# Sixteen copies of the conv's tap rows in DRAM, and half of a weight chunk copied from SBUF by SyncE

## The chip, the cores and the metric

The kernel runs on one core of a Trainium2 chip. The metric is the device time of one execution in microseconds. Several executions are taken and their median is told; one further execution is recorded by the hardware profiler, and every duration of a single instruction comes from that one.

## The reference

A light convolution is followed by a two-layer network with an ELU between its layers.

```python
# x: (8, 4096, 192), weight: (8, 7), w_in: (192, 2048), w_out: (2048, 192)
w = softmax(weight, axis=-1)                        # 8 heads, 7 taps
out[b, s, h, g] = sum_k w[h, k] * x_pad[b, s + k, h, g]   # causal, 24 channels per head
h = out.reshape(32768, 192) @ w_in
g = np.where(h > 0.0, h, np.exp(np.minimum(h, 0.0)) - 1.0)
return g @ w_out                                    # (32768, 192), float32
```

## The kernel before

The 32768 tokens are cut into 32 super-tiles of 1024 tokens (`s`), and each into two groups of 512. The hidden width of 2048 is cut into 16 blocks of 128 (`q`). A step `n = 16 s + q` makes, for both groups (`r` or `u` = 0, 1), the block `H` (three matmuls over 64 rows each, L748), its exponential (ACT, L542), a clamp (POOL, L470), and `gT = max(E - 1, H)` (DVE, L609). The products with `w_out` (L782) follow later in "rounds" that begin at step 12 and are spread among the `H` matmuls of later steps. The lists `ROUNDS`, `CONV_AT` and `EARLY_CONV` fix by hand where each piece stands, and `steps` is the order of all engines' work.

TensorE works on 64 rows at a time, in two row halves. So the weights `w_in` stand twice in SBUF: the rows 0 to 63 of the tile serve group 0, the rows 64 to 127, with the same content, serve group 1. The load runs in three chunks of columns, `WCOLS = ((0, 256), (256, 1024), (1024, 2048))`. Each chunk was loaded twice from DRAM, once for each half, with a cast from float32 to bf16. The chunk `k` counts on the semaphore `s_w[k]`, 16 for each load. `Q_PART` tells which chunk a block needs: the last one serves the blocks 8 to 15, so step 8 is the first to ask for it.

The conv of super-tile 0 is computed at the start from a separate load (`xf`, transposed by TensorE). From super-tile 1 on the conv is a matmul with a banded matrix `Tm` (L726): row `p` of `Tm` holds the taps of all heads, shifted by `p`. To build it, SyncE writes the tap rows into a DRAM tensor `conv_taps`, with zero rows around them (L799, L804), waits for both writes (`s_band`), and reads them back with a stride of -1 element per partition (L809). Before, `conv_taps` held two copies; the read took the partitions 0 to 63 from the one and 64 to 127 from the other:

```python
bass.AP(tensor=taps.tensor, offset=CW + TAP + KSIZE - 1,
        ap=[[(HEADS + 2) * CW - HP, 2], [-1, HP], [1, HEADS * CW]])
```

The conv of super-tile 1 is placed at steps 7 to 10, that of super-tile 2 at steps 13 and 14 (`EARLY_CONV`). Its first matmul waits for `s_band`, and for both halves of `xg`, the tokens of that super-tile. Its result goes through PSUM and ACT into `csb` (L520), and a transposing DMA on SyncE's queue turns it into `att`, the input of the `H` matmuls.

GpSimd's queue issues the casting loads at the start in this order: `w_in` chunk 0 twice, chunk 1 twice, chunk 2 twice, `xg` of super-tile 1 in two halves, `w_out`, `xg` of super-tile 2 in two halves. SyncE's queue issues the tap `weight`, one half of `xf`, the two writes of taps and the band's read; its next instruction is the transpose of super-tile 1. From super-tile 3 on the tokens come from a bf16 copy in DRAM (`x_cast`) that GpSimd's queue writes.

Of the kernel before, what the change touches and what calls it, by code (L numbers as in the profile page):

```python
# [8 lines left out]
BF16 = mybir.dt.bfloat16  # L9
# [3 lines left out]
P = 128  # L13
HP = 64
FC = 128
D = 192
HEADS = 8
KSIZE = 7
# [6 lines left out]
TAP = 6  # L25
# [16 lines left out]
CONV_AT = ((0, 1, 1, 0), (4, 1, 1, 1), (9, 2, 0, 0), (12, 2, 0, 1))  # L42
EARLY_CONV = ((7, 1, 0, 0), (8, 1, 0, 1), (9, 1, 1, 0), (10, 1, 1, 1), (13, 2, 0, 0), (14, 2, 0, 1))
OPS_CONV = 2
FIRST = {}
M_NS, R_NS, C_NS = 215.8, 82.5, 102.5
QUAD = 4
# [6 lines left out]
def bass_lightweight_conv__then__act_elu_kernel(  # L54
# [160 lines left out]
            t, half = divmod(n_half - 1, 2)  # L215
            previous[n_half // 2, n_half % 2, 0, g] = (t, half, 0, g)

    taps = nc.dram_tensor("conv_taps", (2 * (HEADS + 2) * CW,), BF16).ap()

    xb = nc.dram_tensor("x_cast", (NT, D), BF16).ap()  # L220

    with ExitStack() as stack:
# [6 lines left out]
        def sema(name):  # L229
            return stack.enter_context(nc.semaphore(name))  # L230
# [27 lines left out]
        ops = psum("ops", [P, 2, GS])  # L258

        s_w = [sema(f"s_w{i}") for i in range(4)]  # L260
        s_wd = sema("s_wd")
        s_xl = [sema(f"s_xl{i}") for i in range(2)]
        s_xh = sema("s_xh")
# [128 lines left out]
        @block.gpsimd  # L392
        def _gpsimd(g: bass.BassGpSimd):
            W = Waits(g)

            def load_x(s, part):
                g.dma_start(  # L397
                    xg[:, s % NXB, WPG * part : WPG * (part + 1), :],
                    bass.AP(
                        tensor=x_flat.tensor,  # L400
                        offset=(s * SUP + GS * part - PAD) * D,
                        ap=[[D, P], [TOK * D, WPG], [1, D]],
                    ),
                ).then_inc(s_x[s % NXB][part], 16)

            def pad_x(s):
                x_ready(W, s, 0)
                g.memset(xg[0:PAD, s % NXB, 0, :], 0.0).then_inc(s_z)

            def copy_x(s):  # L410
                W(s_cv, 4 * (s - NXB - 1) + 1)
                if s == NXB + 1:
                    g.dma_start(  # L413
                        xb[s * SUP - 8 : s * SUP, :], x_flat[s * SUP - 8 : s * SUP, :]
                    ).then_inc(s_xb[s % 2], 16)
                g.dma_start(  # L416
                    xb[s * SUP : (s + 1) * SUP, :].rearrange("(p t) d -> p (t d)", p=P),
                    x_flat[s * SUP : (s + 1) * SUP, :].rearrange("(p t) d -> p (t d)", p=P),
                ).then_inc(s_xb[s % 2], 16)

            def load_w_in(k, halves):
                c0, c1 = WCOLS[k]
                for r in halves:
                    g.dma_start(  # L424
                        w_in[HP * r : HP * (r + 1), :, c0:c1],
                        moe_w_in.rearrange("(p j) f -> p j f", j=3)[:, :, c0:c1],
                    ).then_inc(s_w[k], 16)

            W(s_one, 1)
            g.affine_select(  # L430
                out=ident[:],
                in_=ident[:],
                pattern=[[-1, P]],
                compare_op=ALU.is_equal,
                fill=0.0,
                base=0,
                channel_multiplier=1,
            ).then_inc(s_id)
            g.affine_select(  # L439
                out=sel[:].rearrange("p (r h c) -> p r h c", r=2, h=HEADS),  # L440
                in_=sel[:].rearrange("p (r h c) -> p r h c", r=2, h=HEADS),
                pattern=[[0, 2], [-1, HEADS], [0, 8]],
                compare_op=ALU.is_equal,
                fill=0.0,
                base=0,
                channel_multiplier=1,
            ).then_inc(s_id)
            W(s_wd, 16)
            load_w_in(0, (0, 1))
            load_w_in(1, (0, 1))  # L450
            load_w_in(2, (0, 1))
            load_x(1, 0)
            load_x(1, 1)
            g.dma_start(
                w_out.rearrange("p (q r) d -> p q (r d)", r=RUN),
                moe_w_out.rearrange("(q p r) d -> p q (r d)", p=FC, r=RUN),
            ).then_inc(s_w[3], 16)
            load_x(2, 0)
            load_x(2, 1)
            for n in range(NP):  # L460
                s, i = divmod(n, NQ)
                if i == X_PAD and s + 2 < NS and (s + 2) % SPB == 0:
                    pad_x(s + 2)
                if i == X_COPY and s and s + 3 < NS:
                    copy_x(s + 3)
                if n == X_LATE[0]:
                    copy_x(3)
                for u in range(2):
                    W(s_exp, 2 * n + u + 1)
                    g.tensor_scalar(  # L470
                        out=E[:, n % NE, u, :],
                        in0=E[:, n % NE, u, :],
                        scalar1=1.0,
                        scalar2=0.0,
                        op0=ALU.min,
                        op1=ALU.max,
                    ).then_inc(s_clp)
# [141 lines left out]
        def _tensor(pe):  # L619
# [75 lines left out]
            for x_, op in enumerate(steps):  # L695
# [42 lines left out]
                elif op[0] == "h":  # L738
                    _, n, r, j = op
                    s, q = divmod(n, NQ)  # L740
                    if n == 0:
                        W(s_ha, (1, 1, 2)[j])
                        W(s_hd, (0, 1, 2)[j])
                    if j == 0:
                        W(s_w[Q_PART[q]], 32)
                        W(s_att[s % 2], 16 * ((s + 1) // 2))
                        wait_bank()
                    ins = pe.matmul(  # L748
                        bank_of(op[:3]),
                        w_in[  # L750
                            HP * r : HP * (r + 1),
                            j,
                            RUN * FC * (q // RUN) + q % RUN : RUN * FC * (q // RUN + 1) : RUN,
                        ],
                        att[HP * r : HP * (r + 1), s % 2, j, 0:GS],
                        start=(j == 0),
                        stop=(j == 2),
                        tile_position=(HP * r, 0),
                    )
                    if j == 2:  # L760
                        ins.then_inc(s_h[r])
                else:
                    _, item, rt, g = op
                    t, half, q, kb, turned = item
                    acc = acc_of(op)
                    W(s_w[3], 16)
                    W(s_tt, 2 * (NQ * t + q) + g + 1)
                    at_end = acc[:2] == (last, 1)
                    if x_ in begins:
                        if at_end:  # L770
                            wait_bank()
                        elif acc in previous:
                            taken(W, previous[acc])
                        else:
                            W(s_ce, 2 * (OPS_CONV - 1) + g + 1)
                    elif steps[seen[acc]][2] != rt:
                        W(s_swap[1 - rt], ends_run[seen[acc]])
                    seen[acc] = x_
                    to = bank_of(("l",) + acc) if at_end else ops[:, g, :]
                    d0 = 0 if at_end else D * kb  # L780
                    t0 = 2 * P * half + P * kb
                    ins = pe.matmul(  # L782
                        to[:, d0 : d0 + D],
                        gT[HP * rt : HP * (rt + 1), t % NG3, q, g, t0 : t0 + P],
                        w_out[HP * rt : HP * (rt + 1), q, :],
                        start=(x_ in begins),
                        stop=(x_ in stops),
                        tile_position=(HP * rt, 0),
                    )
                    if x_ in ends_run:  # L790
                        ins.then_inc(s_swap[rt])

        @block.sync
        def _sync(sy):
# [2 lines left out]
            load_first(sy, 1)  # L797
            W(s_zw, 1)
            sy.dma_start(  # L799
                bass.AP(tensor=taps.tensor, offset=0, ap=[[(HEADS + 2) * CW, 2], [(HEADS + 1) * CW, 2], [1, CW]]),  # L800
                zw[0:2, 0 : 2 * CW].rearrange("p (a e) -> p a e", a=2),
            ).then_inc(s_band, 16)
            W(s_wp, 1)
            sy.dma_start(  # L804
                bass.AP(tensor=taps.tensor, offset=CW, ap=[[CW, HEADS], [(HEADS + 2) * CW, 2], [1, CW]]),
                zt[:, :].unsqueeze(1).to_broadcast([HEADS, 2, CW]),
            ).then_inc(s_band, 16)
            W(s_band, 32)
            sy.dma_start(  # L809
                Tm[:, :, :].rearrange("p h e -> p (h e)"),  # L810
                bass.AP(tensor=taps.tensor, offset=CW + TAP + KSIZE - 1, ap=[[(HEADS + 2) * CW - HP, 2], [-1, HP], [1, HEADS * CW]]),
            ).then_inc(s_band, 16)

            def load_cast(s):
                W(s_cv, 4 * (s - NXB))
# [71 lines left out]
```

## Time and profile before

| | us |
|---|---|
| median of 3 runs | 730.81 (730.28 to 730.85) |
| the profiled execution: its time | 730.68 |
| the profiled execution: its span | 728.6 |
| PE busy | 715.9 |
| ACT, DVE, POOL busy | 656.0, 651.0, 631.0 |
| mean granted clock of TensorE | 0.995 |

The span runs from the first to the last instruction; the rest of the time lies around it. PE stands for TensorE's matmuls and PEld for its weight loads, DVE for VectorE, ACT for ScalarE, POOL for GpSimd, SP for SyncE; a q after an engine's name means the DMA instructions on its queue. In a row of the profile `out<-in` names the tiles, then come the shapes, the number of instructions, their busy time together, the mean of one in ns, and the idle time just before them with what ended most of it. The sizes of DMAs are those at the destination.

### The profile page before, as it was taken

The numbers are of one execution on the slowest core, as the hardware profiler recorded it, in microseconds if no ns is written. First come the engines' busy times: TensorE is split into PE (matmuls) and PEld (weight loads), VectorE is DVE, ScalarE is ACT, GpSimd is POOL, SyncE is SP. The second block draws the span as 40 slices with busy tenths as digits, with TensorE's granted clock in tenths as the row PEclk, the third lists the DMA queues.
The fourth block names the chain that finished last, engine by engine and source line by source line (L and its number), as shares of the span: only waits on it lengthen the run. The fifth ranks groups of instructions, "written<-read, shape, count | busy, mean of one in ns | idle before, by whom it ended". The sixth has DMA issues, their size and how long they took to land.

```text
span 728.6 us, 28723 instructions
## 1 busy us (share of the span) xinstructions
PE 715.9 (98%) x11866; PEld 620.9 (85%) x11866; DVE 651.0 (89%) x1043; ACT 656.0 (90%) x1286; POOL 631.0 (87%) x1078
## 2 busy tenths in 40 slices
PE   8699999999999999999999999999999999999997
PEld 4398888888888888888888888888888888888897
DVE  5599999999999999999999999999999999999994
ACT  6699999999999999999999999999999999999993
POOL 8588888898888898888898888898888898888893
PEclk9899999999999999999999999999999999999999
DMA  9655335455435544335455445355446454532212
GB/s 176 105 102 115 71 93 117 95 91 99 86 95 115 91 94 107 79 93 116 90 95 99 86 95 115 87 99 97 85 97 116 80 105 95 92 93 70 59 35 67
DMA packets 129883, 69.12 MB, mean 95 GB/s; under 512 B 93960, under 2 KB 128520, under 8 KB 129288
## 3 DMA queue, kind: packets, MB, share of 16 engines
q1 hardware_dynamic: 123592, 52.04, 30.3%
q0 software_dynamic: 5872, 14.75, 14.8%
q8 instruction: 93, 1.52, 0.9%
q10 hardware_dynamic: 288, 0.49, 0.2%
q14 instruction: 38, 0.31, 0.1%
HBM read 43.51 MB, written 36.58 MB: 110 GB/s over the span
## 4 chain that ended last, share of the span: by engine, by line
PE 95%; DMA 2%; POOL 1%; ACT 0%; DVE 0%; issue 0%; ACTq 0%
PE ops L782 51%; PE H L748 40%; PE H L726 3%; DMA xg<-in_x_dram 2%; PE H L782 1%; POOL w_in L424 1%; POOL E L470 0%; DVE gT L609 0%; ACT E L542 0%; PE ops L726 0%; POOL xg L397 0%; ACT csb L520 0%; POOL x_cast L413 0%; POOL x_cast L416 0%; POOL sel L439 0%
## 5 line engine op out<-in xcount | busy, mean ns | idle before, releaser
L609 DVE SCALAR_TENSOR_TENSOR gT<-E,H 128x512 f16<-128x512 f32 x1024 | 645.2, 682 | 63.3 <-POOL E L470 56.0
L470 POOL TENSOR_SCALAR E<-E 128x512 f32<-128x512 f32 x1024 | 606.1, 616 | 85.2 <-ACT E L542 81.1
L542 ACT ACTIVATE E<-H 128x512 f32<-128x512 f32 x1024 | 565.0, 611 | 55.5 <-PE H L748 50.7
L748 PE MATMUL H<-att,w_in 64*128 64x512 bf16 x3072 | 604.9, 378 | 1.3 <-DVE gT L609 1.1
L782 PE MATMUL ops<-w_out,gT 64*128 64x192 f16 x8064 | 587.0, 243 | 0.0
L782 PEld LDWEIGHTS ops<-w_out,gT 64*128 64x128 f16 x8064 | 516.4, 94 | 54.5 <-PE ops L782 29.4
L748 PEld LDWEIGHTS H<-att,w_in 64*128 64x128 bf16 x3072 | 258.9, 94 | 20.8 <-DVE gT L609 6.5
L726 PE MATMUL H<-xg,Tm 64*128 64x240 bf16 x480 | 87.6, 263 | 0.3 <-DVE gT L609 0.3
L520 ACT ACTIVATE csb<-H 128x480 bf16<-128x480 f32 x120 | 70.7, 589 | 0.0
L512 ACT ACTIVATE osb<-ops 128x384 f32<-128x384 f32 x125 | 61.0, 488 | 7.3 <-PE ops L782 5.7
L726 PEld LDWEIGHTS H<-xg,Tm 64*128 64x128 bf16 x480 | 38.2, 93 | 16.2 <-issue 0.6
L416 POOL DMA_DIRECT2D x_cast<-in_x_dram x29 | 15.6, 538 | 0.0
L726 PE MATMUL ops<-xg,Tm 64*128 64x240 bf16 x16 | 4.3, 362 | 5.4 <-DMA xg<-in_x_dram 5.4
L726 PEld LDWEIGHTS ops<-xg,Tm 64*128 64x128 bf16 x16 | 1.6, 114 | 7.3 <-issue 5.9
L782 PE MATMUL H<-w_out,gT 64*128 64x192 f16 x128 | 6.4, 243 | 0.0
L782 PEld LDWEIGHTS H<-w_out,gT 64*128 64x128 f16 x128 | 5.7, 94 | 0.0
L637 PE MATMUL ops<-zw 128*128 128x512 bf16 x9 | 3.6, 579 | 1.3 <-DVE zw L552 1.3
L601 DVE COPY osb<-ops 128x384 f32<-128x384 f32 x1 | 0.6, 558 | 4.3 <-PE ops L782 4.3
L698 PE MATMUL ops<-zw 64*128 64x512 bf16 x12 | 4.4, 377 | 0.0
L424 POOL DMA_DIRECT2D w_in<-in_moe_w_in_dram x6 | 3.9, 662 | 0.2 <-DMA wh<-in_weight_dram 0.2
L637 PEld LDWEIGHTS ops<-zw 128*128 128x128 bf16 x9 | 1.2, 141 | 3.2 <-issue 1.9
L397 POOL DMA_DIRECT2D xg<-in_x_dram x4 | 3.5, 878 | 0.0
(49 smaller groups left out, 28.0 us busy)
## 6 DMA issues: line engine op xcount, KB each, us to landing
out_dram<-osb SPq DMA_DIRECT2D x126, 192.0 KB, 3.3
x_cast<-in_x_dram POOLq DMA_DIRECT2D x29, 384.0 KB, 5.3
xg<-x_cast SPq DMA_DIRECT2D x58, 192.0 KB
xg<-x_cast SPq DMA_DIRECT2D x58, 26.2 KB
xg<-in_x_dram POOLq DMA_DIRECT2D x4, 240.0 KB, 17.6
w_in<-in_moe_w_in_dram POOLq DMA_DIRECT2D x2, 384.0 KB, 9.9
w_out<-in_moe_w_out_dram POOLq DMA_DIRECT2D x1, 768.0 KB, 18.9
w_in<-in_moe_w_in_dram POOLq DMA_DIRECT2D x2, 288.0 KB, 6.4
```

What stands on the lines that cost most here:

```text
L416: g.dma_start(xb[s * SUP : (s + 1) * SUP, :].rearrange("(p t) d -> p (t d)", p=P), x_flat[s * SUP : (s + 1) * SUP, :].rearrange("(p t) d - ...
L424: g.dma_start(w_in[HP * r : HP * (r + 1), :, c0:c1], moe_w_in.rearrange("(p j) f -> p j f", j=3)[:, :, c0:c1],).then_inc(s_w[k], 16)
L470: g.tensor_scalar(out=E[:, n % NE, u, :], in0=E[:, n % NE, u, :], scalar1=1.0, scalar2=0.0, op0=ALU.min, op1=ALU.max,).then_inc(s_clp)
L512: a.activation(*out_pieces(acc), ACT.Copy).then_inc(s_oev)
L520: return a.activation(csb[:, s % 2, :].rearrange("p (j v h i) -> p h j v i", j=3, v=2 * WPG, h=HEADS)[:, h0 : h0 + HB], bank_of(("c", m, b ...
L542: a.activation(E[:, n % NE, u, :], bank_of(op[:3]), ACT.Exp).then_inc(s_exp)
L609: v.scalar_tensor_tensor(out=gT[:, s % NG3, q, u, :], in0=E[:, n % NE, u, :], scalar=1.0, in1=bank_of(op[:3]), op0=ALU.subtract, op1=ALU.m ...
L637: pe.matmul(ops[:, 0, :], zw[:, 0:P], zw[:], start=True, stop=True)
L698: pe.matmul(ops[:, 1 - rt, :], zw[HP * rt : HP * (rt + 1), 0:P], zw[HP * rt : HP * (rt + 1), :], start=True, stop=True, tile_position=(HP ...
L726: ins = pe.matmul(bank_of(op[:3])[:, n1 * hh : n1 * (hh + 1)], Tm[HP * rt : HP * (rt + 1), h, :], xg[HP * rt : HP * (rt + 1), s % NXB, :, ...
L748: ins = pe.matmul(bank_of(op[:3]), w_in[HP * r : HP * (r + 1), j, RUN * FC * (q // RUN) + q % RUN : RUN * FC * (q // RUN + 1) : RUN,], att ...
L782: ins = pe.matmul(to[:, d0 : d0 + D], gT[HP * rt : HP * (rt + 1), t % NG3, q, g, t0 : t0 + P], w_out[HP * rt : HP * (rt + 1), q, :], start ...
```

## The change

`conv_taps` holds sixteen copies of the tap rows in place of two, and the band's read takes eight partitions from each. The second load of the last chunk of `w_in` is dropped from GpSimd's queue. In its place SyncE, after the band's read, waits for the first load (`s_w[2]` at 16) and copies the rows 0 to 63 of that chunk to the rows 64 to 127 within SBUF, counted on a new semaphore `s_wc`. The `H` matmuls of group 0 wait for the load, those of group 1 for the copy.

```diff
+BANDS = 16
-    taps = nc.dram_tensor("conv_taps", (2 * (HEADS + 2) * CW,), BF16).ap()
+    taps = nc.dram_tensor("conv_taps", (BANDS * (HEADS + 2) * CW,), BF16).ap()
+        s_wc = sema("s_wc")
             load_w_in(0, (0, 1))
             load_w_in(1, (0, 1))
-            load_w_in(2, (0, 1))
+            load_w_in(2, (0,))
                     if j == 0:
-                        W(s_w[Q_PART[q]], 32)
+                        if Q_PART[q] < 2:
+                            W(s_w[Q_PART[q]], 32)
+                        else:
+                            W(s_wc if r else s_w[2], 16)
             sy.dma_start(
-                bass.AP(tensor=taps.tensor, offset=0, ap=[[(HEADS + 2) * CW, 2], [(HEADS + 1) * CW, 2], [1, CW]]),
-                zw[0:2, 0 : 2 * CW].rearrange("p (a e) -> p a e", a=2),
+                bass.AP(tensor=taps.tensor, offset=0, ap=[[(HEADS + 2) * CW, BANDS], [(HEADS + 1) * CW, 2], [1, CW]]),
+                zw[0:BANDS, 0 : 2 * CW].rearrange("p (a e) -> p a e", a=2),
             ).then_inc(s_band, 16)
             W(s_wp, 1)
             sy.dma_start(
-                bass.AP(tensor=taps.tensor, offset=CW, ap=[[CW, HEADS], [(HEADS + 2) * CW, 2], [1, CW]]),
-                zt[:, :].unsqueeze(1).to_broadcast([HEADS, 2, CW]),
+                bass.AP(tensor=taps.tensor, offset=CW, ap=[[CW, HEADS], [(HEADS + 2) * CW, BANDS], [1, CW]]),
+                zt[:, :].unsqueeze(1).to_broadcast([HEADS, BANDS, CW]),
             ).then_inc(s_band, 16)
             W(s_band, 32)
             sy.dma_start(
                 Tm[:, :, :].rearrange("p h e -> p (h e)"),
-                bass.AP(tensor=taps.tensor, offset=CW + TAP + KSIZE - 1, ap=[[(HEADS + 2) * CW - HP, 2], [-1, HP], [1, HEADS * CW]]),
+                bass.AP(tensor=taps.tensor, offset=CW + TAP + KSIZE - 1, ap=[[(HEADS + 2) * CW - P // BANDS, BANDS], [-1, P // BANDS], [1, HEADS * CW]]),
             ).then_inc(s_band, 16)
+
+            c0, c1 = WCOLS[2]
+            W(s_w[2], 16)
+            sy.dma_start(w_in[HP:P, :, c0:c1], w_in[0:HP, :, c0:c1]).then_inc(s_wc, 16)
```

## The prediction

> **What bounds the kernel now.** I read the page first, then the chain in order of time, the start window by window, and each engine's timeline there. The page:
>
> ```profile
> span 728.6 us, 28723 instructions
> ...
> PE 715.9 (98%) x11866; PEld 620.9 (85%) x11866; DVE 651.0 (89%) x1043; ACT 656.0 (90%) x1286; POOL 631.0 (87%) x1078
> ...
> PEclk9899999999999999999999999999999999999999
> ...
> L748 PE MATMUL H<-att,w_in 64*128 64x512 bf16 x3072 | 604.9, 378 | 1.3 <-DVE gT L609 1.1
> ```
>
> PE is busy 98% of the span. The 12.7 us in which it is idle are all that a change of transfers can win, beside the slice in which its clock was lower. The list of waits puts the largest piece in one place, and the chain says what ended it:
>
> ```profile
> PE ops L726 <- DMA xg<-in_x_dram: 5.4, 1, 5.4
> ```
>
> ```profile
> 7.29 15.86 DMA xg<-in_x_dram
> 23.15 0.14 issue
> 23.28 0.35 PE ops L726
> ```
>
> That is the first conv group (step n = 7), which needs all of `xg` of super-tile 1 and `Tm`. The stretches around it (columns: PE, PEld, DVE, ACT, POOL busy with instruction counts, then the granted clock, DMA share, GB/s):
>
> ```profile
> 10.00:17.90 7.90, 7.51 (x53) 2.26 (x51) 6.01 (x11) 6.70 (x14) 7.29 (x13) 1.00 1.25 201
> 17.90:23.25 5.35, 0.03 (x1) 0.00 (x0) 2.57 (x5) 0.78 (x2) 1.59 (x3) 0.82 1.38 202
> 23.25:28.20 4.95, 4.85 (x30) 2.84 (x30) 1.46 (x3) 3.06 (x6) 2.02 (x4) 0.50 0.27 36
> 28.20:33.00 4.80, 4.01 (x33) 1.64 (x31) 4.10 (x7) 4.68 (x11) 3.83 (x7) 1.00 0.10 19
> 38.00:728.00 690.00, 686.48 (x11585) 605.01 (x11581) 628.27 (x998) 631.86 (x1239) 603.23 (x1029) 1.00 0.44 93
> ```
>
> The reader should see three things. PE stands still for 5.35 us while the DMA engines are fully used. For the 4.95 us after it, it runs at half clock. From 38 us on it has no gap worth the name, so whatever is won before 38 us is passed on whole to the end.
>
> Why is `xg` late? The trace records when each of the 16 DMA engines finishes its share of a transfer. For the second half of `xg`(1), fourteen engines finish between 16.67 and 18.39 us, and two at 22.74 and 23.15. For `Tm` only two finish at all, at 21.55 and 22.02. So the band's read, 128 packets of 2 KB, runs on two engines, 64 packets each. They start at 11.06 us, alternate one for one with the packets of POOL's loads, and delay those loads on these two engines by 23.15 - 18.39 = 4.8 us (74 ns a packet). The other fourteen engines would have let PE go on at 18.4 us.
>
> **The change part by part.**
>
> *Sixteen copies of the taps.* The read's source then has 16 outer rows, not 2. The Trainium skill (DMA: Bandwidth & Descriptors, section "Why a DMA increments its semaphore by 16 and not by 1") says that a transfer uses the largest number of engines up to 16 that divides the slowest dimension on both sides. The rows agree (2 source rows: 2 engines; the 8-row write: 8), and it tells what they cannot: that 16 rows give 16 engines. Then each has 8 packets, 8 x 74 ns = 0.6 us, instead of 64. The gain on the two slow engines is 4.8 - 0.6 = 4.2 us; the others lose 0.6.
>
> The writes grow: 2x2 to 16x2 rows of 256 B, and 8x2 to 8x16 (16 packets on each of 8 engines). The packets of before took 18 to 31 ns, so 16 x 31 = 0.5 us. SP's `Tm` issue, at 5.68, moves to about 6.3. The first packet came 5.4 us after the issue, so packets run from about 11.7 with 246 ns spacing beside `w_in` packets: 8 x 0.25 = 2 us, landing near 14. PE asks at about 17.9. Cost nothing; the cover is 4 us.
>
> *One load less on POOL's queue.* POOL issues one 0.63 us DMA less; it is hidden, since POOL is done issuing at 10.77 and its first clamp starts at 11.38, waiting for ACT. The queue matters: the first half of chunk 2 finishes on the fourteen engines between 12.27 and 13.57, the second between about 14.2 and 16.1. So a half costs about 2.0 us on every engine (12 packets of 173 ns), and all behind it (`xg`(1), `w_out`, `xg`(2)) comes 2.0 us earlier.
>
> *The copy on SP.* It is queued after the band's read and waits for `s_w[2]`: 13.57 + 0.6 = 14.2 us. Behind it on SP stands the first transpose, issued only at 31.38:
>
> ```profile
> SPq L387 <- ACT csb L520: 51.8, 29, 25.0
> ```
>
> SP waited 25.0 us there, so its own wait and issue (0.66 us like `Tm`'s) cost nothing. No row shows a copy from SBUF to SBUF. From above: `Tm`'s latency of 5.4 us, 12 packets per engine at the spacing of `Tm`'s later packets, 123 ns (1.5 us), and 0.5 us to the landing: 14.3 + 7.4 = 21.7. From below: 1.0 us to the first packet, as with the first `xf` load (0.81 to 1.83): 17.3. I take 18.3, nearer the low end: `Tm` stood behind `w_in` packets of 135 ns already taken up, the copy stands behind short `xg` packets, of which 40 pass in 1.1 us.
>
> Here a rule speaks against the change. The same page ("Issuing engines are not separate DMA queues") says that transfers issued by several engines still run on the same 16 and interleave, so moving the load to SP only saves issue time. If so, the 24 KB per engine cost the queue as much as before, and `xg`(1) lands at 18.4 + 0.6 = 19.0: a stall of 1.1 us, gain about 5.5. The trace prices the two differently: a casting packet costs 173 ns, a plain 2 KB one takes 74 from its neighbours, 12 x 74 = 0.9 us, and the copy starts when most of `xg`(1) is through. I take the trace: 18.39 - 2.0 + 0.6 = 17.0, at worst 17.9 with the whole copy ahead. PE arrives at 17.92. The stall is gone.
>
> *New waits on PE.* `H`(8, r=0) waits for the first half (14.2: free), `H`(8, r=1) for the copy; behind it stands all of PE. Natural time of `H`(8,1): ACT's exp pairs come every 1.21 us until n = 6 (at 17.59), then with one evacuation of the conv between them. Two pieces without a gap show the pace:
>
> ```profile
> 28.36 1.08 ACT L542 ACTIVATE E<-H 128x512 f32<-128x512 f32 x2
> 29.34 0.58 ACT L520 ACTIVATE csb<-ops 128x480 bf16<-128x480 f32 x1
> 29.79 1.11 ACT L542 ACTIVATE E<-H 128x512 f32<-128x512 f32 x2
> 30.74 0.61 ACT L520 ACTIVATE csb<-ops 128x480 bf16<-128x480 f32 x1
> 31.19 2.74 ACT L542 ACTIVATE E<-H 128x512 f32<-128x512 f32 x5
> ```
>
> That is 1.42 us per step. Exp(7) at 18.8, exp(8,0) at 20.2, exp(8,1) at 20.8, so its matmuls must start by about 20.1. The copy at 18.3 is in time by 1.8 us; at 21.7 it is late by 1.6.
>
> *The sum.* Before, exp(11) starts at 31.19. After: 18.8 + 4 x 1.42 = 24.5. DVE, which still has work until 20.47, needs 1.28 us per step and cannot start step 11 before 20.5 + 4 x 1.28 = 25.6, where it started at 32.58: 7.0 us at the most. ACT's 6.7, less 0.2 for seams: **6.5 us**, of which 5.36 is the stall and the rest the half clock and refilling. What is late next: `w_out` lands near 21 (step 12 asks at 26), `xg`(2) at 24.82 - 2.0 + 0.6 + 0.9 = 24.3 (step 13 asks at about 26); the transpose had 2.9 us to spare. All hold. The cast copies to DRAM are issued by POOL at step 13 and move along.
>
> Profiled run: 730.68 (span 728.6 and 2.1 around it), 0.13 under the median of 730.81. 730.8 - 6.5 = 724.3.
>
> **The rivals.**
> 1. *The copy is late* (17%): latency like `Tm`'s, 21.7 us or a little more. PE then waits 1 to 2.5 us at step 8. The skill (TensorE: Matmul & The Clock Gate, "What's actually happening") needs an idle window of about 3.4 us before the clock halves; here 5.35 us did it, and no shorter stall shows the threshold. So the clock stays: gain 4 to 5.5, 725.3 to 726.8. Against it: the short packets ahead.
> 2. *The queue frees no time* (6%): the rule above; gain about 5.5, or 4 if `w_out` and `xg`(2) then come late too: 725.3 to 726.8.
> 3. *The band does not spread*, so that the change does not do what it says (3%): the two engines only gain the 2.0 us of the load: landing at 21.2, past the idle window, gain 1 to 2: 729.
> 4. *Slower* (4%): the copy itself runs on two engines, as `Tm` did, 96 packets each at 123 ns = 11.8 us, after 14.3 + 1.0 to 5.4: landing at 27 to 31.5, plus 0.5. It costs from about 26.5 on, where exp(8,1) was fed before: 731 to 736, with the clock halved again. Against it: both sides have 64 partitions outermost.
> 5. *As forecast* (70%): 723.8 to 725.2.
>
> **How the numbers follow.** A measurement of this kernel can tell about 0.2%, 1.5 us. Cases 1, 2 and 5 are faster, and most of 3: 0.93. Around zero: 0.03. Slower: 0.04. The range starts below the bound that DVE sets (7.0 us and 0.4 of scatter: 723.4) and takes in the late copy: 727.0.
>
> **What would show it.** Right: the `xg` wait on PE at 18 us gone; clock 1.00 from 10 to 33 us; exp(11) near 24.5; the transpose issued near 25; `Tm` finished by sixteen engines near 14. Case 1 would be a wait of `H` for `w_in` at 20 us; case 2 an `xg` wait of 1 us; case 3 two late engines again. Wrong altogether if PE gets to 38 us' work earlier by over 6 us and the end does not: then a later stage would hold time that the busy columns hide.

## The result, and the profile after

The changed kernel takes 726.53 us (median of 4; 725.74 to 728.68) where the kernel before takes 730.83. The ratio is 0.9948, with a 95% interval of 0.9926 to 0.9969. A second series on another occasion gave 726.80 and a ratio of 0.9946 (0.9934 to 0.9959). So the gain is real, 3.7 to 4.3 us, and about three fifths of the 6.5 us that were forecast. The profile below is of the fastest of the four executions, 725.74.

The page of the changed kernel, in the lines that answer to those of before (the lines of the source moved by two to five):

```profile
span 723.3 us, 28724 instructions
...
PE 714.9 (99%) x11866; PEld 620.3 (86%) x11866; DVE 651.1 (90%) x1043; ACT 656.1 (91%) x1286; POOL 630.4 (87%) x1077
...
PEclk9999999999999999999999999999999999999999
...
L753 PE MATMUL H<-att,w_in 64*128 64x512 bf16 x3072 | 602.8, 377 | 3.0 <-DVE gT L611 2.5
```

Its list of waits no longer has the 5.4 us for `xg`. In their place stands a wait that was not there before:

```profile
PE H L753 <- DVE gT L611: 2.5, 4, 1.7
...
PEld H L753 <- DMA w_in<-w_in: 1.9, 1, 1.9
```

The two rows are one event. The weight load of an `H` matmul waits 1.9 us for `w_in<-w_in`, the copy. The matmul behind it is idle for 1.7 of them; that row names DVE, which had long been done. The copy lands at 21.58 and the matmul starts at 21.63, so the landing of the copy is the cause. The stretches at the start (columns as before: PE, PEld, DVE, ACT, POOL busy, clock, DMA share, GB/s):

```profile
10.00:17.90 7.90, 7.40 (x57) 2.28 (x53) 5.82 (x11) 6.76 (x13) 6.12 (x12) 1.00 1.30 204
17.90:23.25 5.35, 3.55 (x34) 1.70 (x31) 4.30 (x8) 3.61 (x8) 3.58 (x7) 1.00 1.35 225
23.25:28.20 4.95, 3.98 (x29) 1.43 (x28) 4.12 (x7) 4.95 (x12) 4.20 (x8) 1.00 0.17 23
28.20:33.00 4.80, 4.42 (x76) 3.61 (x74) 3.86 (x7) 3.83 (x8) 4.77 (x9) 1.00 1.11 171
```

In the second stretch PE is busy 3.55 us where it was busy 0.03, and the clock is 1.00 throughout. ACT's timeline shows where the rest was lost:

```profile
18.12 2.28 ACT L544 ACTIVATE E<-H 128x512 f32<-128x512 f32 x4 [0.32 <-PE H L753]
20.29 0.58 ACT L522 ACTIVATE csb<-ops 128x480 bf16<-128x480 f32 x1
22.27 1.09 ACT L544 ACTIVATE E<-H 128x512 f32<-128x512 f32 x2 [1.41 <-PE H L753]
...
26.51 2.78 ACT L544 ACTIVATE E<-H 128x512 f32<-128x512 f32 x5
```

The exponentials of steps 6 and 7 run without a gap, so the conv of step 7 was not late. Those of step 8 come 1.41 us late. Exp(11), the first exponential of step 11, starts at 26.51; it was 31.19 before, and forecast at 24.5. From there the lead is passed on: ACT's last evacuation of `ops` starts at 718.14 in place of 722.79, 4.65 us earlier against 4.68 at step 11. The recorded span gained 5.3 us; the last 0.65 lie in the final writes to DRAM, where SP's first pair takes 1.34 us in place of 2.04, and nothing in the change bears on them.

### The profile page after: what moved, and what is told of

Read it like the earlier page. It is cut to its first block, busy times and chain, and to the rows that moved or that the text cites. A ratio compares the mean times of both kernels' runs of the same rounds, so it can differ in the third digit from the quotient of the medians.

```text
span 723.3 us, 28724 instructions
## 1 busy us (share of the span) xinstructions
PE 714.9 (99%) x11866; PEld 620.3 (86%) x11866; DVE 651.1 (90%) x1043; ACT 656.1 (91%) x1286; POOL 630.4 (87%) x1077
## 4 chain that ended last, share of the span: by engine, by line
PE 96%; DVE 1%; POOL 1%; ACT 1%; issue 0%; ACTq 0%
PE ops L787 51%; PE H L753 40%; PE H L728 3%; DVE gT L611 1%; PE H L787 1%; PE ops L639 1%; POOL E L472 0%; ACT E L544 0%; PE H L683 0%; PE H L663 0%; PE ops L683 0%; ACT csb L522 0%; PE H L650 0%; POOL x_cast L415 0%; POOL x_cast L418 0%
## 5 line engine op out<-in xcount | busy, mean ns | idle before, releaser
L728 PE MATMUL ops<-xg,Tm 64*128 64x240 bf16 x16 | 2.8, 263 | 0.4 <-ACT csb L522 0.4
L522 ACT ACTIVATE csb<-ops 128x480 bf16<-128x480 f32 x4 | 2.4, 605 | 0.0
```

The source lines that it names most:

```text
L522: return a.activation(csb[:, s % 2, :].rearrange("p (j v h i) -> p h j v i", j=3, v=2 * WPG, h=HEADS)[:, h0 : h0 + HB], bank_of(("c", m, b ...
L728: ins = pe.matmul(bank_of(op[:3])[:, n1 * hh : n1 * (hh + 1)], Tm[HP * rt : HP * (rt + 1), h, :], xg[HP * rt : HP * (rt + 1), s % NXB, :, ...
```

## The experiments

Theory A: the band now runs on all engines and `xg` is in time; what is missing is that the copy lands late. Theory B: the copy is neutral and the shortfall lies in the start or the clock. Theories C to F are about two details and come with their runs.

**1. The sixteen copies of the taps alone** (`bands_only`).

```diff
-            load_w_in(2, (0,))
+            load_w_in(2, (0, 1))
-                            W(s_wc if r else s_w[2], 16)
+                            W(s_w[2], 32)
-            sy.dma_start(w_in[HP:P, :, c0:c1], w_in[0:HP, :, c0:c1]).then_inc(s_wc, 16)
```

> Only the sixteen copies of the tap rows; the last chunk of w_in is loaded twice by GpSimd's queue as before. Theory A (the changed kernel falls short because the copy lands late): the two slow engines are gone, xg of super-tile 1 lands at 18.4 + 0.6 = 19.0 us or a little later, TensorE waits 1 to 1.5 us for it at step 7 and for no w_in at step 8; gain over before 5 us, about the time of the changed kernel (726). Rival B (the copy is neutral and the shortfall lies in the start or the clock): the second load's 2.0 us come back whole on top of the changed kernel's time, 728 to 728.5.

726.40 us, ratio 0.9939 (0.9925 to 0.9952). The waits of this kernel:

```profile
PE ops L728 <- DMA xg<-in_x_dram: 1.2, 1, 1.2
```

That is A's forecast, with a gain of 4.1 us where it had 5. As far as these runs can tell (726.40 here, 726.80 for the changed kernel in the series taken with it), spreading the band gives the whole gain of the change. The copy, the other half of it, brings nothing on top: it takes the 1.2 us for `xg` away and puts 1.7 us for itself in their place.

**2. The copy alone** (`copy_only`): `BANDS = 2`, the rest as changed.

> Only the copy in place of the second load; the tap rows have two copies as before. Both theories: the band's read runs on two engines again, so these two finish xg near 23.15 - 2.0 = 21.2 us, and TensorE waits there about 3.3 us. Gain over before 1.5 to 2.5 us (728.5 to 729.3). If the gain were over 4 us, the two engines were never the cause.

731.53 us, ratio 1.0011 (1.0002 to 1.0020): no gain, and a little slower than before. Both theories had forecast a gain, so this is a miss of both. The chain of this kernel, in order of time, ends its long wait later than before (23.15 us) although 2.0 us of packets were taken out:

```profile
6.74 17.81 DMA xg<-in_x_dram
```

`xg` lands at 24.55. The two slow engines finish `Tm` at 21.40 and 22.19, about as late as before (21.55 and 22.02), and have the copy's packets to send after it (they land at 23.95 and 24.38), while `xg` still is in line. Theory C: the packets of the two queues alternate, so that `xg` on these engines is held up by everything on SP's queue. Taking 12 packets away ahead of `xg` then only lets the band meet it sooner. Run 4 tests it.

**3. A small second load, and a copy of the rest** (`small_load_rest_copy`). GpSimd's queue loads the columns of steps 8 and 9 a second time, behind `xg`.

```diff
             load_x(1, 1)
+            g.dma_start(
+                w_in[HP:P, :, WCOLS[2][0] : WCOLS[2][0] + RUN * FC],
+                moe_w_in.rearrange("(p j) f -> p j f", j=3)[:, :, WCOLS[2][0] : WCOLS[2][0] + RUN * FC],
+            ).then_inc(s_ws, 16)
-            c0, c1 = WCOLS[2]
+            c0, c1 = WCOLS[2][0] + RUN * FC, WCOLS[2][1]
-                            W(s_wc if r else s_w[2], 16)
+                            W((s_ws if q < 8 + RUN else s_wc) if r else s_w[2], 16)
```

> As the changed kernel, but the first 256 columns of the last chunk (steps 8 and 9) are loaded a second time by GpSimd's queue behind xg of super-tile 1, and only the other 768 columns are copied. Theory A: the columns land near 18.3 us, the wait of 1.7 us on TensorE at step 8 is gone, step 10 asks for the copy after 22.5 us and finds it; 1.5 us faster than the changed kernel, 724.5 to 725.2. Rival B: the same time as the changed kernel within 0.5 us.

724.27 us (forecast 724.5 to 725.2), ratio 0.9915 (0.9901 to 0.9928). Its interval lies below that of the changed kernel's second series, which was taken together with it. The wait is gone, and the exponentials of step 8 follow without a gap:

```profile
17.85 2.28 ACT L549 ACTIVATE E<-H 128x512 f32<-128x512 f32 x4 [0.33 <-PE H L758]
20.02 0.58 ACT L527 ACTIVATE csb<-ops 128x480 bf16<-128x480 f32 x1
20.47 1.11 ACT L549 ACTIVATE E<-H 128x512 f32<-128x512 f32 x2
21.42 0.61 ACT L527 ACTIVATE csb<-ops 128x480 bf16<-128x480 f32 x1
21.87 1.14 ACT L549 ACTIVATE E<-H 128x512 f32<-128x512 f32 x2
```

The pace is 1.40 us per step, as the forecast had it (1.42), and exp(11) starts at 24.68 (forecast 24.5), 1.83 us earlier than in the changed kernel. Of these, 0.28 lie in the start, since exp(0) begins at 10.93 in place of 11.21; the other 1.55 are the late copy. So A holds against B, which had the same time as the changed kernel within 0.5 us. This kernel is faster than the changed one, and in its median faster than run 1 (726.40), though their intervals touch.

**4. Two copies of the taps, no copy in SBUF, the second load behind `xg`** (`two_bands_load_after`).

> Two copies of the tap rows, no copy in SBUF, the second load behind xg of super-tile 1. It asks why the copy alone gained nothing. Theory C (on the two slow engines packets of the two queues alternate one for one, so xg cannot end before the 64 packets of the band, and the copy adds 12 more behind them): without the copy the band's read ends near 21.5 us, xg near 22; gain over before 1 to 2 us, 728.5 to 729.5. Rival D (the copy is not the reason, the band's read alone holds xg up as long): as before and as the copy alone, 730.3 to 731.5.

729.18 us, ratio 0.9981 (0.9973 to 0.9990), in C's range. Now PE waits 4.0 us for `xg`, where it waited 6.5 in run 2 and 5.4 before:

```profile
PE ops L732 <- DMA xg<-in_x_dram: 4.0, 1, 4.0
```

On the two slow engines the band's read ends at 20.53 and 21.70, and `xg` at 21.31 and 22.33. The last is 2.2 us earlier than with the copy. Two readings follow. First, `xg` ends 0.6 to 0.8 us behind the band here and 2.4 to 2.7 us behind it in run 2, so the copy's 12 packets cost it about 1.7 to 2.0 us; the rest is that the band itself ended later there. Second, the 2.0 us of packets taken out ahead bring `xg` only 0.8 us (23.15 to 22.33), because the band ends only 0.3 us earlier on the slower engine (22.02 to 21.70), and it began 0.3 us earlier too. C is supported, and D, which had no gain, is not; that it is the alternation that does it is read from the spacing of the packets, not tried by itself.

**5. The second load behind `xg`, sixteen copies, no copy in SBUF** (`load_after_xg`).

```diff
             load_x(1, 1)
+            g.dma_start(
+                w_in[HP:P, :, WCOLS[2][0] : WCOLS[2][1]],
+                moe_w_in.rearrange("(p j) f -> p j f", j=3)[:, :, WCOLS[2][0] : WCOLS[2][1]],
+            ).then_inc(s_wc, 16)
-            sy.dma_start(w_in[HP:P, :, c0:c1], w_in[0:HP, :, c0:c1]).then_inc(s_wc, 16)
```

> Sixteen copies of the tap rows; no copy in SBUF: the second load of the last chunk stays on GpSimd's queue, but behind xg of super-tile 1. Theory A (what the changed kernel lacks is only the copy's late landing): xg lands as in the changed kernel near 17.5 us, the second load 2.0 us after it, near 19.6; TensorE waits at step 8 for 0 to 0.4 us; 724.5 to 725.3, about as the kernel with the small load. Rival B (the load costs its 2.0 us wherever it stands, since w_out and xg of super-tile 2 come later): 726 to 727.

724.61 us, ratio 0.9922 (0.9908 to 0.9935), in A's range: the order of the queue alone does what the copy was to do. The profiled execution was one of the longer ones, 725.58. In it one engine was late with all its work, and PE waited for it twice:

```profile
PE H L757 <- DMA w_in<-in_moe_w_in_dram: 1.4, 1, 1.4
PE ops L732 <- DMA xg<-in_x_dram: 0.7, 1, 0.7
```

The first wait is the one for chunk 1, from 12.27 to 13.63, and the second the one for `xg` at step 7, which landed at 19.91 in place of 17.5. The second load of the last chunk landed at 21.33 in place of 19.6, and still no wait for it shows at step 8.

**6. Four copies of the taps** (`bands_four`): `BANDS = 4`, otherwise as in run 1.

> As the kernel with the sixteen copies alone, but with four copies: the read's source has 4 outer rows. Theory C: four engines carry 32 packets each, 24 of them beside packets of the last chunk at 246 ns and 8 beside xg's at 124: the read ends near 18, and what is left of xg near 20; TensorE waits 1 us longer than with sixteen copies, 727.0 to 728. If the number of engines did not follow the outer rows: as with two copies (730.5) or as with sixteen (726.4).

727.25 us, ratio 0.9950 (0.9935 to 0.9965).

```profile
PE ops L728 <- DMA xg<-in_x_dram: 3.1, 1, 3.1
```

The trace has four landings for `Tm`, at 17.92 to 18.91, and four late ones for `xg`, the last at 21.12 (forecast 20). PE waits 3.1 us, 1.9 more than with sixteen copies where 1 was forecast. So the engines follow the outer rows of the read: 2, 4 and 16 rows were tried, an engine then has 64, 32 and 8 packets of the band, and the wait goes 5.4, 3.1, 1.2 us. That is 72 to 79 ns for each packet taken off an engine, against the 74 of the prediction.

**7. `w_out` and the next `xg` issued late** (`late_w_out`): the three issues moved from the start of GpSimd's queue to step 8 of its loop, the rest as changed.

```diff
             for n in range(NP):
                 s, i = divmod(n, NQ)
+                if n == 8:
+                    g.dma_start(
+                        w_out.rearrange("p (q r) d -> p q (r d)", r=RUN),
+                        moe_w_out.rearrange("(q p r) d -> p q (r d)", p=FC, r=RUN),
+                    ).then_inc(s_w[3], 16)
+                    load_x(2, 0)
+                    load_x(2, 1)
```

> As the changed kernel, but w_out and xg of super-tile 2 are issued only at step 8 by GpSimd's queue, so that behind xg of super-tile 1 nothing stands in that queue. It asks why the copy's first packet comes 3.9 us after its issue. Theory E (the engines work off packets of GpSimd's queue that they have taken up before): first packet 1 to 2 us after the issue, landing near 18, no wait for it at step 8. Rival F (a copy of this shape on SyncE's queue has that delay by itself): first packet still near 3.9 us after the issue, landing 20 to 20.5. The total time says nothing: w_out comes late to step 12 and the clamps are held up by three issues at step 8.

734.68 us, one execution; as said ahead of the run, the total decides nothing here. The row of the copy among the DMA issues (size, us from issue to landing), in the changed kernel:

```profile
w_in<-w_in SPq DMA_DIRECT2D x1, 384.0 KB, 6.8
```

In this one:

```profile
w_in<-w_in SPq DMA_DIRECT2D x1, 384.0 KB, 3.8
```

In the changed kernel the copy is issued at 14.76 and its first packet starts at 18.75, 4.0 us later. Here it is issued at 17.54 (the whole start was late in this execution) and the first packet comes at 18.86, 1.3 us later. So F is refuted: the copy does not have the long delay by itself, and 2.7 of the 4.0 us go with the packets of GpSimd's queue. Which of them is open, because two things differ from the changed kernel: `w_out` and the next `xg` are not in line, and the late issue comes when much of `xg` of super-tile 1 has already landed. E's picture, that each engine first works off what it has taken up, is not shown either. In the changed kernel the engines end `xg` over 1.8 us (15.72 to 17.49), and yet the copy lands on all sixteen within 0.3 us (21.31 to 21.58). The landing at 21.38 missed "near 18", since the issue itself came late; no wait for the copy at step 8 shows, as forecast.

**8. The changed kernel again** (`after_again`).

> The changed kernel once more, for its scatter. Theory A: 725.5 to 727, TensorE's wait for the copy again 1.5 to 2.5 us; an execution above 728 shows a granted clock under 1.00, one below 726 does not. Rival B: times spread although the clock is the same.

726.80 us (726.09 to 727.57). The copy is issued at 15.69 and lands at 22.57, 6.9 us later. The waits:

```profile
PEld H L753 <- DMA w_in<-w_in: 2.4, 1, 2.4
PE H L753 <- DMA w_in<-w_in: 2.2, 1, 2.2
PEld H L753 <- DMA w_in<-in_moe_w_in_dram: 1.7, 1, 1.7
PE H L753 <- DMA w_in<-in_moe_w_in_dram: 1.2, 1, 1.2
```

In this execution one engine was late already with chunk 1 (13.20 us; 12.33 in the first profile, 11.69 before), and the copy, which waits for the slowest engine of the load, was 0.9 us later too. The row of 1.2 us is PE's wait for chunk 1. The clock was at half for one stretch, shown in the last section. Over both series of the changed kernel, the four executions with a granted clock of 1.000 took 725.74 to 726.80 us, and the five with 0.995 to 0.999 took 726.40 to 728.68. So the clock goes with a part of the scatter; how large a part stays open.

## Why the prediction was right or wrong

- *What bounds it.* Right: the stall at step 7 came from two engines that carried the band's read. With four and sixteen rows it shrank with the packets per engine (run 6), and sixteen rows took off the 4.2 us that were forecast: 5.4 to 1.2 us in run 1.
- *The band.* Right: `Tm` lands on sixteen engines between 13.66 and 15.40 us. The last is 1.4 us later than the forecast "near 14", which is unseen, since PE asks at about 17.9; so are the 0.6 us that the larger writes cost on SP.
- *The load taken out.* Right in the changed kernel: `xg`(1) lands at 17.49, forecast 17.0, at worst 17.9; run 1, which keeps the load, has it at 19.54, and the difference is the 2.0 us of the forecast. The rule that a move to another queue frees no time was rightly set aside for `xg`, but the copy did not run beside the queue for free: it is the copy that came late.
- *The copy.* This is the step that failed. Of the bounds 17.3 and 21.7 I took 18.3, and 21.58 was measured. Its terms: the semaphore at 14.74 (forecast 14.2); issue to first packet 4.0 us (taken 2.0, with an upper end of 5.4); first to last packet 1.9 (1.5); to the landing 0.9 (0.5). The large miss is the second. The argument for the low end was that only short `xg` packets stood ahead, 40 of which pass in 1.1 us. In the profile before, the two halves of `xg`, 40 packets an engine each, land 1.3 us apart. And by the forecast's own times `xg` was in line until 17.0, 2.7 us after the issue, and `w_out` after it. Run 7 has neither `w_out` nor most of `xg` in line at the issue, and there the term is 1.3 us. How the queue holds the copy up stays open.
- *The sum.* Exp(11) came at 26.51, 2.0 us after the forecast. The copy is 1.5 of them (the pair of step 8 was forecast at 20.2, which the later start makes 20.7; it came at 22.27). The other 0.53 is the start: exp(0) began at 11.21 in place of 10.68, because the clock reached full speed only at 7.05 us and not at 4.28. In the ten profiles exp(0) begins the later, the later the clock is full: at 10.68 with 4.28, at 10.90 to 10.97 with 5.3 to 5.8, at about 11.2 with 6.6 to 7.1. So it is scatter of the execution, and the profile of before, the earliest of the ten, was a lucky one that I took as the rule. Before the change such a delay would not have shown, since PE stood waiting for `xg` until 23.15 anyway; with the stall gone it counts.
- *The rivals.* Case 1, the late copy, is what happened, with its time (725.3 to 726.8) and its wait. It had 17%, and the likeliest case 70%; with bounds of 17.3 and 21.7 around a deadline of 20.1, and the latency of the band's read as the only measured one beside loads, the late end deserved the larger share. Its claim that the clock stays up during such a wait held in the first profile of the changed kernel and failed in the second (run 8).
- *The range.* Both medians lie in it, because it was drawn to take in the late copy. Its upper end of 727.0 took the late copy alone; single executions with a lower clock or a slow engine besides, as the profiled one of run 8 (727.24), lie above it.
- *Case 3.* Its landing of 21.2 was too early and its 729 us too low: with the band on two engines, packets taken out ahead hardly come off `xg` (run 4), and the copy's packets come on top. Run 2 is this case, and there `xg` landed at 24.55 and the time was 731.53.

## What to carry to other kernels

Before you count the engines' bandwidth, look at how many engines a transfer lands on: a read with a short outer dimension can hold up every other transfer that shares its two engines. A copy that replaces a load is not free of the load's queue: price it from its issue, with what is already in line, up to its landing (6.8 us here), and set that against the time at which its reader asks. Here it was better to change the order of the loads (run 5), or to load the small part that is needed first and copy the rest (run 3).

## What the hardware showed that was not expected

The clock of TensorE fell to half although PE had not stood idle for the whole time before; the prediction had reckoned with a whole idle window. In run 8 PE was busy 1.24 of 3.41 us, and the next 3.41 us ran at 0.50 (stretches as above):

```profile
19.44:22.85 3.41, 1.24 (x14) 0.46 (x11) 3.24 (x6) 1.80 (x4) 2.31 (x4) 1.00 1.34 238
22.85:26.26 3.41, 3.41 (x24) 1.94 (x22) 1.28 (x2) 2.62 (x6) 1.58 (x3) 0.50 0.46 54
```

The ten profiles together show more. In each, the clock changes only at whole steps of 3.41 us from the moment at which it first was full: before the change it is full at 4.28, at half at 21.35 (5 steps later) and full again at 28.18 (2 steps later). Cut into these steps, a profile shows the clock fall after every step at full clock in which PE was busy 1.33 us or less (seven steps: 0, 0, 0.01, 0.99, 1.04, 1.25 and 1.33 us), and after none in which it was busy 1.99 us or more; no step lies between. In run 8 the wait of 2.2 us fell into one step. The wait of 1.7 us in the first profile of the same kernel lay across the border of two, at 20.70, which left 2.35 and 2.12 us of work in them, and the clock stayed up. So it matters not only how long a wait is, but also where it falls.

The copy's packets, 2 KB from SBUF to SBUF, took 153 ns each with nothing beside them (run 7), one about every 160 ns on an engine. With `w_out`'s packets between them (the changed kernel) each took 96 ns, one about every 150 ns. The band's packets of the same size from DRAM came every 123 ns with another queue's packets between them.
